# One transfer for the output projection's rows, a filler matmul, shared constants, and an uneven split of the result's columns in a gated decode step

## Chip, cores and metric

The kernel runs on one core of one Trainium2 chip. The metric is the device time of one execution in microseconds (us), as the median of several. A profiled execution gives the trace; its span, from the first to the last instruction, is about 1.5 us shorter than the device time. Every execution also has its span (to 0.1 us) recorded.

Engines: PE = TensorE matmul, PEld = its weight loads, DVE = VectorE, ACT = ScalarE, POOL = GpSimd, SPq = the queue of SyncE, which issues the transfers.

## The reference

```python
x = A_x                                              # (1, 1, 576), bf16
g = sigmoid((x * gate_w).sum(-1, keepdims=True))
# A: 32 query heads, 16 key/value heads, the last 4096 of 32768 positions
q = (x @ wq).reshape(1, 1, 32, 128).transpose(0, 2, 1, 3)
p = softmax(einsum("bhqd,bhkd->bhqk", q, k) * 128 ** -0.5)
a = einsum("bhqk,bhkd->bhqd", p, v) ... @ wo         # wo: (4096, 576)
# B: gelu MLP, hidden size 4608
b = gelu(x @ w1 + b1) @ w2 + b2                      # w2: (4608, 576)
return g * a + (1 - g) * b                           # (1, 1, 576), bf16
```

One token, so every weight and every cached key and value is read once and used once: 53.6 MB in, 1152 bytes out.

## The kernel before

Only what the change and the argument touch; `...` marks cuts. The result row of 576 columns accumulates in PSUM as two halves: `y_ps[0:1, ...]` and `y_ps[32:33, ...]`. `y_add` multiplies one vector by one row of `wo` or `w2` and issues a *pair* of matmuls, one for each half. There are 18 + 4 + 31 + 18 such rows: the first half of w2, a "tail" of four output rows, 31 main output rows, the second half of w2.

```python
DH = D // 2                                   # 288
one_b = const.tile([1, 2], BF16)              # a one, memset on POOL
...
xs_ps[:, i, :] <- lhsT=xdup[...], rhs=one_b[0:1, 0:1]     # nine matmuls, spread x over partitions
...
y_out = (y_ps[0:1, 0:DH], y_ps[32:33, 512 : 512 + DH])

def y_add(vec, row, start=False, stop=False):
    for s in range(2):
        last = nc.tensor.matmul(y_out[s], lhsT=vec, rhs=row[:, s * DH : (s + 1) * DH], ...)
    return last
...
for r0, r1 in ((0, 16), (16, RO)):            # RO = 31 rows for each of 128 partitions
    nc.sync.dma_start(out=wo_t[:, r0:r1, :]..., in_=wo_src[...][:, :, r0 * D : r1 * D])
for j0, j1 in ((0, 10), (10, 16), (16, 18)):
    nc.sync.dma_start(out=w2_t[:, NJ + j0 : NJ + j1, :], in_=w2_src[:, 1, j0:j1, :])
...
late = [(gt, f, w2_t[:, f, :]) for f in range(6, NJ)]
late += [(ov_tail, j, wo_tail[:, j, :]) for j in range(4)]
late += wo_at[0:8] + wo_at[16:RO] + wo_at[8:13] + w2_at[0:10] + wo_at[13:16] + w2_at[10:]
# every y_add is ordered behind the one before it
...
nc.scalar.copy(out=out_row[:, DH:D], in_=y_out[1])
nc.vector.tensor_copy(out=out_row[:, 0:DH], in_=y_out[0])
nc.sync.dma_start(out=out..., in_=out_row[:])
```

## Time and profile before

| | before |
|---|---|
| device time, first 3 runs | 131.78 us (131.72 to 132.05) |
| span of the profiled run | 130.1 us |
| busy: PE, DVE, ACT, POOL | 79.7, 52.3, 8.3, 9.2 us |
| bytes read, packets of the loads | 53.6 MB, 2490 |
| last packet of the loads ends | 127.50 us |
| PE ends, store issued | 128.4, 128.96 us |

To read it: add up no busy times. The loads fill their 16 engines for 96.5% of the span, so the table's last two rows are what counts: when the last bytes come, and what has to follow. The lines that show this stand in the prediction.

### The profile page before, as it was taken

Reading aid. Unit: us, or ns where it says so; the run is one execution under the profiler, and the core shown is the slowest. Engines: PE = TensorE matmul, PEld = TensorE weight load, DVE = VectorE, ACT = ScalarE, POOL = GpSimd, SP = SyncE. Lnnn points to the kernel's source line nnn. Section 1 sums busy time; section 2 is a strip of 40 time slices with the busy share of each in tenths; the row PEclk is TensorE's granted clock in tenths of the full one; section 3 lists DMA queues with packets and bytes.
Section 4 is the critical chain, followed back from the end, with each engine's and each line's share of the span. In section 5 each row is a group of like instructions: output and inputs, shape, how many; then the busy total and the mean of one; then the engine's idle time right before and its main releaser. Section 6 shows DMA issues by size and latency. Waiting matters only on the chain.

```text
span 130.1 us, 2403 instructions
## 1 busy us (share of the span) xinstructions
PE 79.7 (61%) x1148; PEld 45.6 (35%) x1077; DVE 52.3 (40%) x48; ACT 8.3 (6%) x18; POOL 9.2 (7%) x26
## 2 busy tenths in 40 slices
PE   0037999476003998939918994995300830899573
PEld 0037679375000121201211120595300830855441
DVE  0153000400079959999999995614000020010001
ACT  2000000003000000030003003011000000000001
POOL 7039700000000000000000000000000000000000
PEclk9999999999999999999997799985555555559999
DMA  6999999799899999999899899899899899999980
GB/s 232 427 431 432 476 424 476 344 484 448 373 458 453 403 433 463 393 433 484 373 433 484 383 423 484 357 432 505 368 433 489 363 438 415 442 401 427 413 363 33
DMA packets 2508, 53.75 MB, mean 413 GB/s; under 512 B 286, under 2 KB 290, under 8 KB 580
## 3 DMA queue, kind: packets, MB, share of 16 engines
q1 hardware_dynamic: 2490, 53.61, 96.5%
q8 instruction: 8, 0.13, 0.4%
q10 hardware_dynamic: 10, 0.01, 0.0%
HBM read 53.62 MB, written 0.00 MB: 412 GB/s over the span
## 4 chain that ended last, share of the span: by engine, by line
DMA 52%; DVE 24%; PE 14%; issue 6%; SPq 2%
DMA k_t<-in_A_k_cache_dram 27%; DMA w_t<-in_B_w_dram 25%; DVE kt L531 19%; PE s_ps L553 7%; PE o_ps L640 5%; DVE m L569 3%; DVE pt L602 2%; PE y_ps L396 1%; SPq L684 1%; DVE mr L572 1%; SPq L691 0%; DVE out_row L736 0%; SPq L234 0%; SPq L230 0%; PE mt_ps L578 0%
## 5 line engine op out<-in xcount | busy, mean ns | idle before, releaser
L553 PE MATMUL s_ps<-kt,qz_flat 128*128 128x512 bf16 x128 | 32.9, 414 | 17.2 <-DVE kt L531 10.4
L531 DVE STREAM_TRANSPOSE kt<-k_t 128x4096 f32<-128x4096 f32 x8 | 35.3, 4433 | 12.2 <-DMA k_t<-in_A_k_cache_dram 10.5
L640 PE MATMUL o_ps<-pt,v_t 128*128 128x8 bf16 x512 | 14.2, 168 | 16.6 <-DMA v_t<-in_A_v_cache_dram 14.7
L553 PEld LDWEIGHTS <-qz_flat 128*128 128x128 bf16 x64 | 6.9, 107 | 40.6 <-issue 40.4
L640 PEld LDWEIGHTS <-v_t 128*128 128x128 bf16 x512 | 14.0, 102 | 17.3 <-DMA v_t<-in_A_v_cache_dram 14.9
L424 PEld LDWEIGHTS <-w_t 128*128 128x128 bf16 x162 | 10.3, 167 | 1.8 <-issue 1.8
L424 PE MATMUL h_ps<-x,w_t 128*128 128x2 bf16 x162 | 10.5, 202 | 0.0
L590 ACT ACTIVATE p_t<-s_ps,negm 128x1024 bf16<-128x1024 f32 x4 | 4.5, 1114 | 50.9 <-DVE negm L586 50.9
L396 PE MATMUL y_ps<-w_t,gt 128*1 128x288 bf16 x72 | 6.3, 329 | 1.2 <-DMA w_t<-in_B_w_dram 1.2
L670 DVE RECIPROCAL rg<-mt_ps 128x32 f32<-128x32 f32 x1 | 0.4, 358 | 15.6 <-PE mt_ps L665 15.6
L602 DVE STREAM_TRANSPOSE pt<-p_t 128x1024 bf16<-128x1024 bf16 x4 | 4.9, 1225 | 2.7 <-ACT p_t L590 2.7
L462 PE MATMUL q_ps<-x,wq_t 128*128 128x2 bf16 x144 | 4.0, 166 | 2.9 <-DMA wq_t<-in_A_wq_dram 2.9
L569 DVE TENSOR_REDUCE m<-s_ps 128x1 f32<-128x1024 f32 x4 | 4.8, 1196 | 1.1 <-PE s_ps L553 1.1
L396 PE MATMUL y_ps<-wo_t,ov 128*1 128x288 bf16 x62 | 4.3, 285 | 1.4 <-DMA wo_t<-in_A_wo_dram 1.4
L736 DVE CAST out_row<-y_ps 1x288 bf16<-1x288 f32 x1 | 0.4, 445 | 11.6 <-PE y_ps L396 11.6
L433 DVE COPY hacc<-h_ps 128x36 f32<-128x36 f32 x1 | 0.2, 196 | 11.9 <-PE h_ps L424 11.9
L462 PEld LDWEIGHTS <-wq_t 128*128 128x128 bf16 x144 | 3.9, 104 | 3.0 <-DMA wq_t<-in_A_wq_dram 3.0
L345 PE MATMUL xs_ps<-one_b,rows 1*128 1x1 bf16 x9 | 0.7, 196 | 6.9 <-DVE rows L339 6.9
L396 PEld LDWEIGHTS <-gt 128*1 128x1 bf16 x72 | 3.3, 92 | 3.4 <-issue 1.6
L694 DVE TENSOR_TENSOR om<-o_ps,rgh 128x128 bf16<-128x128 f32 x1 | 0.3, 291 | 8.6 <-PE o_ps L640 8.6
L396 PEld LDWEIGHTS <-ov 128*1 128x1 bf16 x62 | 2.6, 83 | 2.8 <-issue 1.9
L339 DVE COPY rows<-rows 1x1152 bf16<-1x1152 bf16 x1 | 0.7, 748 | 6.1 <-DMA rows<-in_A_x_dram 6.1
(72 smaller groups left out, 35.5 us busy)
## 6 DMA issues: line engine op xcount, KB each, us to landing
k_t<-in_A_k_cache_dram SPq DMA_DIRECT2D x4, 4096.0 KB, 32.1
v_t<-in_A_v_cache_dram SPq DMA_DIRECT2D x4, 4096.0 KB, 22.8
wq_t<-in_A_wq_dram SPq DMA_DIRECT2D x1, 4608.0 KB, 25.8
w_t<-in_B_w_dram SPq DMA_DIRECT2D x1, 2880.0 KB, 14.1
w_t<-in_B_w_dram SPq DMA_DIRECT2D x1, 2592.0 KB, 22.9
w_t<-in_B_w_dram SPq DMA_DIRECT2D x1, 2304.0 KB, 8.1
wo_t<-in_A_wo_dram SPq DMA_DIRECT2D x1, 2304.0 KB
wo_t<-in_A_wo_dram SPq DMA_DIRECT2D x1, 2160.0 KB
```

Source lines behind the costliest of these rows:

```text
L339: nc.vector.tensor_copy(out=xdup.rearrange("p (d t) -> p d t", t=2), in_=x_row.rearrange("p (d o) -> p d o", o=1).to_broadcast([1, D, 2]),)
L396: last = nc.tensor.matmul(y_out[s], lhsT=vec, rhs=row[:, s * DH : (s + 1) * DH], start=start, stop=stop, skip_group_check=True,)
L424: nc.tensor.matmul(h_ps[:, j:NF:NJ], lhsT=w1_t[:, i, j:FH:NJ], rhs=x2[:, i, :], start=False, stop=(i == NI - 1 and j == NJ - 1), skip_grou ...
L462: nc.tensor.matmul(q_ps[:, j : Hq : Hq // 2], lhsT=wq_t[:, i, j * Dh : (j + 1) * Dh], rhs=x2[:, i, :], start=(i == 0 and j == 0), stop=(i ...
L531: lambda: nc.vector.transpose(out=kt[g, f][:].bitcast(FP32), in_=keys.rearrange("p c d -> p (c d)").bitcast(FP32),),
L553: last = nc.tensor.matmul(s_ps[g][:, u * 512 : (u + 1) * 512].rearrange("p (c k) -> p c k", k=32), lhsT=qz(g, j, 2 * f + half), rhs=kv[:, ...
L569: queue("dve", lambda: nc.vector.reduce_max(out=m1[:], in_=s_ps[g][:], axis=AX.X))
L572: lambda: nc.vector.tensor_scalar(out=mr[:], in0=hi16[:], scalar1=m1[:, 0:1], scalar2=None, op0=ALU.mult),
L590: nc.scalar.activation(out=p_t[:].rearrange("p c k -> p (c k)"), in_=s_ps[g][:], func=ACT.Exp, bias=negm[:, 0:1], scale=SCALE, accum_out=s ...
L602: lambda: nc.vector.transpose(out=pt[:, g, :, :].rearrange("p c q -> p (c q)"), in_=p_t[:].rearrange("p c k -> p (c k)"),),
L640: last = nc.tensor.matmul(o_ps[:, 8 * g : 8 * g + 8, 0], lhsT=v_t[g][:, c, :], rhs=pt[:, g, c % 32, 8 * (c // 32) : 8 * (c // 32) + 8], st ...
L684: nc.sync.dma_start(out=wo_t[:, r0:r1, :].rearrange("p r n -> p (r n)"), in_=wo_src[:, 0 : 4 * RW, :].rearrange("h (a r) n -> h a (r n)", ...
```

## The change

Its intent, as far as the code tells it: fewer and larger transfers, fewer small constants, and a smaller share for the VectorE, whose copy of 288 columns took 445 ns against the ScalarE's 390. The output rows come in one transfer, so they run as one block after it, and a dummy fp32 matmul (the filler) fills the place of the eight rows that used to run ahead.

```diff
-    DH = D // 2
+    DH = 272
...
-    one_b = const.tile([1, 2], BF16, name="one_b")
-    nc.gpsimd.memset(one_b[:], 1.0)
...
-    row_of = const.tile([HB, 16, HB, 2], BF16, name="row_of")
-    nc.gpsimd.memset(row_of[:], 0.0)
+    row_of = zeros[0:HB, ROWS : ROWS + 32 * HB].rearrange(...)     # part of the zeros tile
...
-            rhs=one_b[0:1, 0:1],
+            rhs=ident[0:1, 0:1],
...
-                rhs=row[:, s * DH : (s + 1) * DH],
+                rhs=row[:, DH:D] if s else row[:, 0:DH],
...
-    for r0, r1 in ((0, 16), (16, RO)):
-        nc.sync.dma_start(... r0 * D : r1 * D ...)
+    nc.sync.dma_start(out=wo_t..., in_=wo_src[:, 0 : 4 * RW, :]...)
...
-    late += wo_at[0:8] + wo_at[16:RO] + wo_at[8:13] + w2_at[0:10] + wo_at[13:16] + w2_at[10:]
+    spare_ps = ps_s.tile([P, 1024], FP32, name="spare_ps", tag="s")
+    late.append(None)                     # becomes one 128x512 fp32 matmul into spare_ps
+    late += wo_at + w2_at
```

More of the change, by code (lines that the diff above doesn't have):

```diff
@@ L265 @@
     NZ = 512 + 5 * RW + 1 + 64
-    zeros = const.tile([P, NZ + 4 * D], BF16, name="zeros")
+    ROWS = NZ + 4 * D
+    zeros = const.tile([P, ROWS + 32 * HB], BF16, name="zeros")
     nc.gpsimd.memset(zeros[:].bitcast(FP32), 0.0)
@@ L314 @@
     same8 = is0[:, c0 + 16 : NCC]
-    row_of = const.tile([HB, 16, HB, 2], BF16, name="row_of")
-    nc.gpsimd.memset(row_of[:], 0.0)
+    row_of = zeros[0:HB, ROWS : ROWS + 32 * HB].rearrange("p (r b m) -> p r b m", r=16, b=HB)
     nc.gpsimd.affine_select(
-        out=row_of[:],
-        in_=row_of[:],
+        out=row_of,
+        in_=row_of,
         pattern=[[0, 16], [-1, HB], [0, 2]],
@@ L391 @@
     y_ps = ps_y.tile([64, 1024], FP32, name="y_ps")
-    y_out = (y_ps[0:1, 0:DH], y_ps[32:33, 512 : 512 + DH])
+    y_out = (y_ps[0:1, 0:DH], y_ps[32:33, 512 : 512 + D - DH])
     def y_add(vec, row, start=False, stop=False):
@@ L541, in score_products @@
                     s_ps[g][:, u * 512 : (u + 1) * 512],
-                    lhsT=row_of[:].rearrange("p r b m -> p (r b m)"),
+                    lhsT=row_of.rearrange("p r b m -> p (r b m)"),
                     rhs=foreign[:].rearrange("p n b -> p (n b)"),
@@ L682 @@
     wo_t = big.tile([P, RO, D], BF16, name="wo_t", tag="D")
-    for r0, r1 in ((0, 16), (16, RO)):
-        nc.sync.dma_start(
-            out=wo_t[:, r0:r1, :].rearrange("p r n -> p (r n)"),
-            in_=wo_src[:, 0 : 4 * RW, :].rearrange("h (a r) n -> h a (r n)", a=4)[
-                :, :, r0 * D : r1 * D
-            ],
-        )
+    nc.sync.dma_start(
+        out=wo_t[:].rearrange("p r n -> p (r n)"),
+        in_=wo_src[:, 0 : 4 * RW, :].rearrange("h (a r) n -> h a (r n)", a=4),
+    )
     for j0, j1 in ((0, 10), (10, 16), (16, 18)):
@@ L727 @@
     late += [(ov_tail, j, wo_tail[:, j, :]) for j in range(4)]
-    late += wo_at[0:8] + wo_at[16:RO] + wo_at[8:13] + w2_at[0:10] + wo_at[13:16] + w2_at[10:]
+    spare_ps = ps_s.tile([P, 1024], FP32, name="spare_ps", tag="s")
+    late.append(None)
+    late += wo_at + w2_at
     before = ov_mm
-    for n, (vec, at, row) in enumerate(late):
+    for n, item in enumerate(late):
         with tc.issue_after(before.ins):
+            if item is None:
+                before = nc.tensor.matmul(
+                    spare_ps[:, 0:512],
+                    lhsT=ones[:],
+                    rhs=p_t[:].rearrange("p c k -> p (c k)").bitcast(FP32),
+                    start=True,
+                    stop=True,
+                )
+                continue
+            vec, at, row = item
             before = y_add(vec[:, at : at + 1], row, stop=(n == len(late) - 1))
```

## The prediction

> **What bounds the kernel now.** I read the page first, and on it the row of DMA shares. From the second slice to the last but one the 16 DMA engines are full, and one queue carries nearly everything:
>
> ```profile
> DMA  6999999799899999999899899899899899999980
> PEclk9999999999999999999997799985555555559999
> q1 hardware_dynamic: 2490, 53.61, 96.5%
> ```
>
> 53.61 MB on 16 engines that are 96.5% busy over a span of 130.1 us: whatever the compute engines do, the span cannot get much shorter than the bytes. So the kernel is bound by its transfers, and a change is worth what it does to the transfers, plus what it does behind the last one. The second row matters later: the granted matmul clock is half from about 88 to 117 us and full in the last four slices.
>
> Next the chain that ended last, in order of time, at its end. It says the same: a weight piece that had been waiting in the queue for 33 us, then sixteen matmuls and the copy of the result.
>
> ```profile
> 94.29 32.93 DMA w_t<-in_B_w_dram
> 127.22 0.04 issue
> 127.27 1.19 PE y_ps L396 x16
> 128.45 0.43 DVE out_row L736
> ```
>
> Third the timeline of the last 12 us, because the change reorders exactly these instructions:
>
> ```profile
> 118.58 0.65 PE L396 MATMUL y_ps<-zeros,ov_tail 48*1 48x288 bf16 x8
> 119.16 1.14 PE L396 MATMUL y_ps<-wo_t,ov 128*1 128x288 bf16 x16
> ...
> 121.72 2.61 PE L396 MATMUL y_ps<-wo_t,ov 128*1 128x288 bf16 x40 [1.42 <-DMA wo_t<-in_A_wo_dram]
> ...
> 125.18 1.39 PE L396 MATMUL y_ps<-w_t,gt 128*1 128x288 bf16 x20 [0.84 <-DMA w_t<-in_B_w_dram]
> ...
> 126.40 0.54 PE L396 MATMUL y_ps<-wo_t,ov 128*1 128x288 bf16 x6
> ...
> 127.27 1.15 PE L396 MATMUL y_ps<-w_t,gt 128*1 128x288 bf16 x16 [0.33 <-DMA w_t<-in_B_w_dram]
> ...
> 128.44 0.45 DVE L736 CAST out_row<-y_ps 1x288 bf16<-1x288 f32 x1 [11.62 <-PE y_ps L396]
> 128.48 0.39 ACT L735 CAST out_row<-y_ps 1x288 bf16<-1x288 f32 x1 [11.47 <-PE y_ps L396]
> 128.96 0.28 SPq L737 DMA_DIRECT2D out_dram<-out_row  x1
> ```
>
> Four idle gaps follow landings: the second half of the output projection at 121.72, the first w2 piece (ten rows) at 125.18, the second (six rows) at 127.27. The PE is not the bound here: it idles 1.42 + 0.84 + 0.33 = 2.59 us in the last 10.
>
> The trace also lists every packet. The last 2304-byte packet (third w2 piece, two rows) ends at 127.50 us. Packets of the three pieces before it end 0.48 to 0.50 us before the PE is let go (121.23 against 121.72, 124.68 against 125.18, 126.78 against 127.27), so the third piece is usable at about 127.99. The PE, starting six rows at 127.27, gets to its rows at 127.27 + 6 x 0.1225 = 128.00. Both are equally late: second and third piece bind together, within 0.01 us.
>
> **What the Trainium skill says.** "TensorE: Matmul & The Clock Gate", section "Back-to-back issue gap", gives N / 2.4 + 2.5 ns for one matmul at full clock, so 122.5 ns for 288 columns. The trace agrees for a *pair*: 20 pairs in 2.61 us is 20 x 122.5 ns plus 0.16 for the last to drain, 10 pairs in 1.39 and 8 in 1.15 fit with the same 0.16. The two matmuls of a pair therefore run at once; section "Part 3: Packing small matmuls — row/col tiling" of that page says outputs at partitions 0 and 32 fall in separate column groups, and that is how y_ps is laid out. Part 1 of the page says that the clock halves after an idle window of about 3.4 us; in this trace the step up comes at 117.6 us, 3 us into the burst that starts at 114.62. "DMA: Bandwidth & Descriptors", section "Rules for kernel authors", advises to coalesce small transfers, and says that below 64 KB one mostly pays overhead. The two halves merged here are 2304 and 2160 KB, so the advice gives almost nothing: 2304-byte packets take 94 ns and 32768-byte packets 1218 ns on average, which is 0.0369 ns per byte and about 9 ns fixed per packet.
>
> **The change part by part.** *One transfer for 31 rows.* Before: 128 packets of 18432 B and 128 of 17280 B; after: 128 of 35712 B, the same bytes. On each of 16 engines that is 8 packets fewer and one 4-byte semaphore packet fewer (those take 9 ns): 9 x 9 = 0.08 us off everything that lands behind. Issues are also fewer (0.58 us each), but the queue is 30 us ahead of the data, so that is hidden. I take 0.08 us off each landing: rows at 121.64, w2 pieces at 125.10, 127.19 and 127.91.
>
> *The order of the tail.* The eight output rows (16 matmuls) that ran at 119.16 now wait for the whole transfer, and a filler of 128x512 fp32 takes their place. After the landing the PE has 31 + 10 + 8 = 49 pairs.
>
> *The split 272 to 304.* A pair now lasts as long as its longer half: 304 / 2.4 + 2.5 = 129.2 ns (an estimate with the skill's formula that fitted above), 6.7 ns more. Walk: 121.64 + 31 x 0.1292 = 125.65 (first w2 piece long there); + 10 x 0.1292 = 126.94; wait for 127.19; + 6 x 0.1292 = 127.97 (third piece there at 127.91); + 2 x 0.1292 + 0.16 = 128.39. Before it was 128.42. So of the 49 x 6.7 = 0.33 us that the split costs, the eight last pairs' 0.05 lie on the path; the rest, and the eight rows moved back (8 x 0.129 = 1.03 us), eat the idle time of 0.84 + 0.33. What is left is 0.25 us.
>
> *The result's copies.* Slopes from this trace: DVE casts from PSUM take 190 ns for 31 columns and 445 for 288, so 1.0 ns a column; ACT 180 ns for 32 and 390 for 288, so 0.8. DVE gets 445 - 16 = 429, ACT 390 + 13 = 403. The ACT starts 0.04 later. Ends before: 128.89 and 128.87; after, relative to the same PE end: 128.87 and 128.88. Gain 0.01 us.
>
> *The constants.* The one-element operand of the first nine matmuls becomes the identity's corner. That is a new wait:
>
> ```profile
> 6.90 0.69 PE L345 MATMUL xs_ps<-one_b,rows 1*128 1x1 bf16 x9 [6.90 <-DVE rows L339]
> ...
> 9.34 0.29 POOL masks.py:199 TENSOR_SCALAR_AFFINE_SELECT ident<-ident 128x128 bf16<-128x128 bf16 x1
> ...
> 27.00 4.00 PE L462 MATMUL q_ps<-x,wq_t 128*128 128x2 bf16 x144 [2.87 <-DMA wq_t<-in_A_wq_dram]
> ```
>
> They now start at about 9.65 instead of 6.90. The bias matmuls that follow were at 10.49 and the w1 products at 11.70; nine matmuls (0.69) and the gate's (0.55) from 9.65 give 10.9 for the first and 12.2 for the second, some 0.5 us later. The PE then waits 2.87 us for wq at 24.13 to 27.00, which swallows it. The GpSimd saves two memsets (0.09 and 0.19 us) and spends about 0.06 on a wider one; nothing waits for them at the end.
>
> Sum: -0.03 at the PE end (0.08 off the landings, 0.05 back for wider pairs), -0.01 at the copies: 0.04 us. From 131.78 that is 131.74; as the best guess I take 131.70, since removing a boundary between transfers may also trim the spread between engines (the third w2 piece ends at 127.24 on the earliest of its sixteen last packets and 127.50 on the latest), which the packet sum does not count.
>
> **The rivals.** *The PE becomes the bound.* If the whole projection lands 0.25 us later relative to the w2 pieces, or a pair costs 135 instead of 129 ns, the slack of 0.25 us after 41 pairs is gone and each further 0.1 us shows in full. For it: 49 pairs now follow one landing. Against: the landing was measured for the last half, and the end of one transfer in ring order is the end of the same bytes. Time: 131.9 to 132.1.
>
> *The clock falls.* Without the filler the PE would idle from 119.2 to 121.6. If it went to half, pairs would take 304 / 1.2 = 253 ns for up to 3.4 us: 13 pairs' worth, about 1.7 us, less 0.25 slack: 133.2. Against: the filler. The fp32 bias pair of 576 columns took 1.12 us at 15.2 us, from which I estimate 1.0 to 1.9 us for the filler, so the idle is at most 1.5 us, as before (1.42), and the PE is busy for most of the time around it. Should the filler last 1.9 us from 119.4, it still ends at 121.3, ahead of the rows.
>
> *The transfer gain is real and larger*, for instance because the queue switches slowly between transfers. For it: nothing in the packet list; packets follow each other closely. It would make 131.3.
>
> **Range and chances.** The three runs before spread by 0.33 us, more than the effect. The mechanisms known add up to under 0.1 us, the two plausible surprises are +0.2 and -0.3. I give 131.70 with 131.35 to 132.00. A move by 2% is 2.6 us: only a fallen clock comes half that far. Faster 0.01, same 0.98, slower 0.01.
>
> **What would show it.** Right: in the new timeline the output rows run as one block of 62 matmuls at about 121.6 lasting 4.1 us, no idle before the first w2 piece's rows, a short wait (0.2 to 0.3) before the last sixteen, these lasting about 1.2 us; the last 2304-byte packets end under 0.1 us earlier; the clock stays full from 117.6 to the end; the q_ps block still starts at 27.0. Wrong: a wait of zero there and a later end (PE-bound), a half clock after 120 us, or landings that move by over 0.2 us.

## The result

| | before | changed | ratio of the fast runs |
|---|---|---|---|
| first series, 6 runs each | 131.80 us (131.64 to 132.05) | 131.68 us (131.52 to 131.88) | 0.9991, 95% interval 0.9978 to 1.0004 |

"Same", and inside the range of 131.35 to 132.00; the point was 131.70. A ratio is the mean time of one kernel's fast runs over that of the other's of the same rounds, so not quite the ratio of the medians beside it.

The page of the changed kernel, its clock row and its main queue. There are 144 packets fewer (2346 for 2490) and the same bytes:

```profile
PEclk9999999999999999999995899975555555555999
q1 hardware_dynamic: 2346, 53.61, 96.4%
```

The chain that ended last (start, duration, what), at its end. It has the shape of the one before: a w2 piece, sixteen matmuls, a copy. But the last copy is now the ScalarE's:

```profile
94.69 32.72 DMA w_t<-in_B_w_dram
127.41 0.04 issue
127.45 1.21 PE y_ps L394 x16
...
128.69 0.40 ACT out_row L742
```

The timeline of the last 13 us (start, duration, engine, line, what):

```profile
116.85 3.20 PE L394 MATMUL y_ps<-w_t,gt 128*1 128x272 bf16 x24
...
119.98 0.75 PE L394 MATMUL y_ps<-zeros,ov_tail 48*1 48x272 bf16 x8
...
120.66 1.13 PE L730 MATMUL spare_ps<-p_t,ones 128*128 128x512 f32 x2
...
121.90 3.78 PE L394 MATMUL y_ps<-wo_t,ov 128*1 128x272 bf16 x59
...
125.49 0.28 PE L394 MATMUL y_ps<-w_t,gt 128*1 128x272 bf16 x1
125.52 0.29 PE L394 MATMUL y_ps<-wo_t,ov 128*1 128x304 bf16 x1
...
128.57 0.43 DVE L743 CAST out_row<-y_ps 1x272 bf16<-1x272 f32 x1 [11.43 <-PE y_ps L394]
128.69 0.40 ACT L742 CAST out_row<-y_ps 1x304 bf16<-1x304 f32 x1 [11.35 <-PE y_ps L394]
129.12 0.28 SPq L744 DMA_DIRECT2D out_dram<-out_row  x1
```

And the groups of that stretch with shapes kept apart (count, then busy us and mean ns of one):

```profile
L394 PE MATMUL y_ps<-wo_t,ov 128*1 128x304 bf16 x31 | 4.2, 292 | 0.0
L394 PE MATMUL y_ps<-wo_t,ov 128*1 128x272 bf16 x31 | 3.8, 279 | 0.1
```

Four things to see. First, the long idle gaps before the output rows and before the first w2 piece are gone; the wait that is left is the one at 127.45. Second, the two halves of the row run at their own pace: 31 matmuls of 272 columns are busy for 3.8 us, 31 of 304 for 4.2, and a w2 matmul of the narrow half starts at 125.49, ahead of output-row matmuls of the wide half (125.52) that come before it in program order. The lead has a limit: the narrow half never starts more than four rows ahead, and its last two rows before the wait go at the wide half's 0.129 us instead of 0.116. Third, the copies therefore start 0.12 us apart and the ScalarE's ends last: 128.57 + 0.43 = 129.00 against 128.69 + 0.40 = 129.09. Fourth, the clock stepped up at 120.17 us, not at 117.57 as in the trace before, so the filler ran at 120.66 to 121.79, right up to the rows.

The span of this profile is 0.2 us longer than that of before, while its time in the series is 0.1 us shorter. The last packet of the loads ends at 127.62 against 127.50. Over nine profiles of kernels with the one transfer (the changed kernel three times, and six profiles of variants below that leave the loads alone) this end lies between 127.47 and 127.69. That is the trace's own spread, over twice the effect in question; so single profiles tell mechanisms here, not 0.1 us.

### The profile page after: what moved, and what is told of

Its sections match the earlier page's. It is cut to its first block, busy times and chain, and to the rows that moved or that the text cites. A ratio compares the mean times of both kernels' runs of the same rounds, so it can differ in the third digit from the quotient of the medians.

```text
span 130.3 us, 2402 instructions
## 1 busy us (share of the span) xinstructions
PE 81.5 (63%) x1150; PEld 47.8 (37%) x1080; DVE 52.0 (40%) x48; ACT 8.3 (6%) x18; POOL 9.1 (7%) x24
## 2 busy tenths in 40 slices
DMA packets 2364, 53.75 MB, mean 413 GB/s; under 512 B 270, under 2 KB 274, under 8 KB 564
## 3 DMA queue, kind: packets, MB, share of 16 engines
q1 hardware_dynamic: 2346, 53.61, 96.4%
## 4 chain that ended last, share of the span: by engine, by line
DMA 52%; DVE 24%; PE 13%; issue 6%; SPq 2%; ACT 0%
DMA k_t<-in_A_k_cache_dram 27%; DMA w_t<-in_B_w_dram 25%; DVE kt L529 19%; PE s_ps L551 7%; PE o_ps L638 5%; DVE m L567 3%; DVE pt L600 2%; SPq L686 1%; PE y_ps L394 1%; DVE mr L570 1%; SPq L681 0%; PE mt_ps L576 0%; SPq L234 0%; ACT out_row L742 0%; SPq L230 0%
## 5 line engine op out<-in xcount | busy, mean ns | idle before, releaser
L551 PE MATMUL s_ps<-kt,qz_flat 128*128 128x512 bf16 x128 | 32.4, 410 | 17.4 <-DVE kt L529 10.6
L394 PE MATMUL y_ps<-w_t,gt 128*1 128x272 bf16 (+1 forms) x72 | 8.0, 363 | 0.1
L343 PE MATMUL xs_ps<-ident,rows 1*128 1x1 bf16 x9 | 0.6, 189 | 9.4 <-POOL ident masks.py:199 9.4
L394 PEld LDWEIGHTS <-gt 128*1 128x1 bf16 x72 | 4.5, 97 | 2.2 <-issue 0.7
L394 PE MATMUL y_ps<-wo_t,ov 128*1 128x272 bf16 (+1 forms) x62 | 4.2, 286 | 0.1
L343 PEld LDWEIGHTS <-rows 1*128 1x128 bf16 x9 | 0.7, 150 | 9.3 <-DVE rows L337 6.6
L394 PEld LDWEIGHTS <-ov 128*1 128x1 bf16 x62 | 3.4, 84 | 1.3 <-issue 0.8
```

The source lines that it names most:

```text
L343: nc.tensor.matmul(xs_ps[:, i, :], lhsT=xdup[:, i : 2 * D : NI], rhs=ident[0:1, 0:1], start=(i == 0), stop=(i == NI - 1), skip_group_check ...
L394: last = nc.tensor.matmul(y_out[s], lhsT=vec, rhs=row[:, DH:D] if s else row[:, 0:DH], start=start, stop=stop, skip_group_check=True,)
L551: last = nc.tensor.matmul(s_ps[g][:, u * 512 : (u + 1) * 512].rearrange("p (c k) -> p c k", k=32), lhsT=qz(g, j, 2 * f + half), rhs=kv[:, ...
```

## The experiments

Twelve experiments with nine different kernels, in three jobs on three chips, five rounds each, all correct. "Before" and the ratios below are of the kernel before in the same job. The three series of the changed kernel against the kernel before:

| series | changed, median | before, median | ratio, 95% interval |
|---|---|---|---|
| first | 131.68 us | 131.80 us | 0.9991 (0.9978 to 1.0004) |
| control | 131.73 us | 131.78 us | 0.9992 (0.9974 to 1.0009) |
| control_2 | 131.69 us | 131.72 us | 0.9990 (0.9976 to 1.0005) |

**control** and **control_2**: no edit.

> The changed kernel once more, for a second profile and a tighter interval. Theory (the transfers bind the end, one boundary less is worth 0.08 us, the wider pairs cost back 0.05): ratio to the kernel before 0.9995 to 1.000. Rival (the boundary between two transfers is worth more than its packets): 0.997 or less. The landing of the last w2 piece varies by 0.1 us from profile to profile, and the clock step up falls where its 3.4 us grid lies.

> The changed kernel once more, beside the next three on one chip. Spans of 130.1 to 130.4 us in all six runs; with the filler no run shows a span over 131.

Three series agree on 0.1% less by their means, 0.12 us, and none excludes zero. By the medians it is 0.12, 0.05 and 0.03 us; the means of the kernel before hold a few long times (132.12 to 132.32) whose spans are ordinary (130.2 to 130.5). The spans of control_2 are 130.1 to 130.4, of control 130.2 to 130.3; none of the 17 runs is above 131. The small gain fits the packet count but is not shown by timing; the next two runs enlarge its cause instead.

### What a packet costs

**row_packets**: one transfer for the output rows as changed; the four w2 transfers are rewritten, as the program is finished, to one run per row.

```diff
 src, dst = i.ins[0], i.outs[0]          # of each w2 load: 128 partitions x (rows * 576)
+rows_ap = [[D, size // D], [1, D]]
+ins=[copy.replace(src, ap=[src.ap[0]] + rows_ap)], outs=[copy.replace(dst, ap=[dst.ap[0]] + rows_ap)]
```

> One transfer for the output rows as changed, but the four w2 transfers cut into packets of one row (1152 B): 288 packets on each engine in place of 32, no transfer more. Theory: 256 x 9 ns = 2.3 us over the changed kernel, all at the landing of the last piece. Rival (packets of over 512 B are free): nothing.

**eight_transfers** and **two_transfers**:

```diff
-    nc.sync.dma_start(out=wo_t..., in_=wo_src...)
+    for r0, r1 in ((0, 4), (4, 8), ..., (24, 28), (28, RO)):     # two_transfers: ((0, 16), (16, RO))
+        nc.sync.dma_start(out=wo_t[:, r0:r1, :]..., in_=...[:, :, r0 * D : r1 * D])
```

> The output rows in eight transfers (seven of 4 rows, one of 3): 56 data packets and 7 semaphore packets more on each engine than in one. Theory: 63 x 9 ns = 0.57 us over the changed kernel. Rival (cost sits in the boundary, say 0.2 us each): 1.4 us or more. Rival (hidden): nothing.

> The changed kernel with the output rows in two transfers again (16 and 15 rows), order, filler and split as changed. Theory (9 ns a packet, 9 packets more on each engine): 0.08 us over the changed kernel. Rival (a boundary costs more than its packets): 0.3 us or more.

| | median | before | ratio, 95% interval |
|---|---|---|---|
| two_transfers | 131.75 us | 131.70 us | 1.0002 (0.9990 to 1.0014) |
| eight_transfers | 132.22 us | 131.70 us | 1.0037 (1.0024 to 1.0050) |
| row_packets | 133.88 us | 131.70 us | 1.0174 (1.0159 to 1.0188) |

The page of row_packets shows that the edit did what it should: 4096 packets more than the 2364 of the changed kernel, the same bytes.

```profile
DMA packets 6460, 53.75 MB, mean 406 GB/s; under 512 B 270, under 2 KB 4882, under 8 KB 4916
```

From two transfers to eight there are 48 data and 6 semaphore packets more on each engine: 54 x 9 ns = 0.49 us; measured 132.22 - 131.75 = 0.47. From two_transfers to row_packets there are 256 - 9 = 247 more: 2.2 us; measured 2.13. So the boundaries between transfers show no price beyond their packets (to about 0.2 us for six of them, which is what the intervals resolve), packets of over 1 KB are not free, and what the loads lose the time loses in full. So the one transfer should be worth 9 x 9 = 0.08 us. Against two_transfers the changed kernel's ratio in its first series, another job, is 0.0011 lower (0.14 us), with intervals that overlap: compatible, not resolved.

**one_w1**: the same gain sought at the other end of the queue, as a version that might beat both kernels.

```diff
-    for i0, i1 in ((0, 4), (4, NI)):
+    for i0, i1 in ((0, NI),):
         nc.sync.dma_start(out=w1_t[:, i0:i1, :], in_=w1_src[:, i0:i1, :])
```

> The changed kernel with the w1 rows in one transfer instead of two (128 packets of 41472 B in place of 128 of 18432 and 128 of 23040). Theory (9 packets less on each engine, 9 ns each, at the start of a queue that never runs dry): 0.08 us less than the changed kernel, and the w1 products start at about 15 instead of 11.5 and end at about 25.3, still ahead of wq at 27.0. Rival (the late start of the products reaches the end): 0.3 us or more over it.

131.72 us, ratio 0.9995 (0.9982 to 1.0008), spans 130.2 to 130.4: as the changed kernel. My expectation of the products was wrong, for they started at 20.21 us and ended at 30.4, not at 25.3, and ran past the landing of wq. Yet nothing reached the end: the copies of the queries (qz_flat) ended at 35.96 us and the score products that need them started at 41.35, so even then the early chain had over 5 us of room. A gain of 0.08 us isn't visible, nor excluded.

### The shared constant

**own_one**:

```diff
+    one_b = const.tile([1, 2], BF16, name="one_b")
+    nc.gpsimd.memset(one_b[:], 1.0)
-            rhs=ident[0:1, 0:1],
+            rhs=one_b[0:1, 0:1],
```

> The changed kernel with the one-element constant given back to the first nine matmuls. Theory: they start at 6.6 us instead of 9.4, the q_ps block still starts at 27.0, and the time is that of the changed kernel within 0.05 us. Rival (the early chain reaches the end): 0.3 us or more less.

131.69 us, the changed kernel's median within 0.05 us as expected; ratio 1.0009 (0.9992 to 1.0026), with one run of 132.39 whose span is ordinary (130.4). Timeline lines, first of the changed kernel, then of own_one:

```profile
9.40 0.64 PE L343 MATMUL xs_ps<-ident,rows 1*128 1x1 bf16 x9 [9.40 <-POOL ident masks.py:199]
26.97 4.00 PE L460 MATMUL q_ps<-x,wq_t 128*128 128x2 bf16 x144 [2.95 <-DMA wq_t<-in_A_wq_dram]
```

```profile
7.30 0.69 PE L345 MATMUL xs_ps<-one_b,rows 1*128 1x1 bf16 x9 [7.30 <-DVE rows L339]
26.89 4.00 PE L462 MATMUL q_ps<-x,wq_t 128*128 128x2 bf16 x144 [2.45 <-DMA wq_t<-in_A_wq_dram]
```

The shared constant costs 2.1 us of waiting at the start, and the wait for wq swallows all of it. The move of `row_of` into the zeros tile was not tested by itself; it changes GpSimd work before 15.2 us, in front of the same wait.

### The split

**wide_split**:

```diff
-    DH = 272
+    DH = 224
```

> The changed kernel with columns 224 to 352. Theory (a pair lasts as long as its longer half, 352 / 2.4 + 2.5 = 149 ns): 49 pairs from 121.85 us end at 129.3 instead of 128.65, with 0.04 us more for the copy: 0.6 to 0.7 us over the control, and the wait before the last sixteen matmuls is gone in the ScalarE's half. Rival (a pair lasts as the mean of its halves): no change.

132.68 us (132.36 to 133.51), ratio 1.0071 (1.0044 to 1.0098). Three of six runs lie at 132.36 to 132.52, 0.6 to 0.8 over the control's 131.73; three at 132.85 to 133.51. The profile is of the second sort (132.98):

```profile
121.35 1.12 PE L730 MATMUL spare_ps<-p_t,ones 128*128 128x512 f32 x2
...
129.77 0.38 DVE L743 CAST out_row<-y_ps 1x224 bf16<-1x224 f32 x1 [12.43 <-PE y_ps L394]
129.91 0.44 ACT L742 CAST out_row<-y_ps 1x352 bf16<-1x352 f32 x1 [12.38 <-PE y_ps L394]
```

Its clock stepped up only at 120.61 us, the longer pairs had made the work before late, and the filler held the PE until 122.40, when the rows had long landed (last packet 121.33). From there 49 x 0.1492 + 0.16 us give 129.87 for the wide half, and its copy starts at 129.91. So the longer half sets the end, the mean does not, and with no slack left each delay shows in full. The narrow half went at 96 ns a row for twelve rows, until it was four rows ahead, and from there at the wide half's 149 ns.

**even_split**, run twice:

```diff
-    DH = 272
+    DH = D // 2
```

> The changed kernel with columns 288 to 288. Theory: the two column groups run at their own pace, the end waits for the slower; with 288 the ScalarE's half ends 8 x 6.7 = 0.05 us earlier behind the last wait, so 0.05 us less than the control (ratio to it 0.9996), and the two copies start within 0.05 us of each other instead of 0.12. Rival (the split serves its purpose): 0.05 us more than the control.

> 288 to 288 again, because the first time its four ordinary runs were 0.13 us over the control, which its trace does not explain: from the last wait of the PE to the end of the later copy both take 1.62 us (0.05 us less matmul, 0.05 us more for the VectorE's copy). Theory now: equal, medians within 0.06 us of control_2. Rival (the split gains 0.1 us): again 0.1 or more over it.

First series 131.89 us, ratio 1.0025 (0.9991 to 1.0059); second 131.86 (131.82 by its fast runs), ratio 1.0015 (0.9985 to 1.0046). The first expectation, 0.05 us *less* than the control, fell: the median is 0.16 us over it. The second, within 0.06 us of control_2, missed too: 0.13 us over it by the fast runs, as the rival said. The first trace gives no reason for such a difference:

```profile
127.50 1.15 PE L394 MATMUL y_ps<-w_t,gt 128*1 128x288 bf16 x16 [0.37 <-DMA w_t<-in_B_w_dram]
...
128.68 0.45 DVE L743 CAST out_row<-y_ps 1x288 bf16<-1x288 f32 x1 [11.59 <-PE y_ps L394]
128.72 0.39 ACT L742 CAST out_row<-y_ps 1x288 bf16<-1x288 f32 x1 [11.43 <-PE y_ps L394]
```

From the wait's end to the end of the later copy it is 129.13 - 127.50 = 1.63 us here, 129.09 - 127.45 = 1.64 with 272 to 304, and 128.89 - 127.27 = 1.62 in the kernel before. What the narrow half gains for the VectorE, the wide half's matmuls take. So the trace argues for no effect, and the timing neither shows nor excludes that the uneven split gains 0.1 us: the ordinary runs of the second series (131.58 to 131.89) lie as control_2's (131.56 to 131.82), those of the first (131.80 to 131.89) above the control's (131.67 to 131.77), and the intervals overlap.

The second series' profiled run is slow (134.22) and is no measure of the split. But its trace shows where this one run lost its time, and it was not in the loads, whose last packet ended at 127.49:

```profile
121.22 2.07 PE L730 MATMUL spare_ps<-p_t,ones 128*128 128x512 f32 x2
...
123.22 5.16 PE L394 MATMUL y_ps<-wo_t,ov 128*1 128x288 bf16 x62
```

Its clock stood at half until 125.71 us. At half clock the filler took 2.07 us instead of 1.13 and held the output rows until 123.22, while their last packet had come at 121.21.

Two other runs of the twelve were long: 133.31 and 132.95, with spans of 131.9 and 131.5 us. They pull the ratios up. They were not profiled, so whether the clock did it there too is not known. The changed kernel has no such run in 17; whether 288 columns make them likelier stays open with three cases.

### The filler

**no_filler**, run twice:

```diff
-    spare_ps = ps_s.tile([P, 1024], FP32, name="spare_ps", tag="s")
-    late.append(None)
```

> The changed kernel without the 128x512 fp32 filler. Theory: the idle before the output rows is 1 to 2.5 us, under one 3.4 us window, the clock stays full or has just risen, and the end is set by the transfers: within 0.1 us of the control. Rival (the filler is needed): the clock is half after 121.8 us, 62 matmuls take 6 to 8 us instead of 4.1, and the time is 1 to 1.7 us longer.

> Without the filler again, for the share of runs in which the clock falls. The first time 2 of 6 runs had a span of 131.5 and more, and the one that was profiled shows the clock at half from 122.24 to 125.66. Theory now (the idle of 1.6 us is shorter than a 3.4 us grid cell, so a fall depends on where the grid lies): again some of the six runs at 131.4 to 131.7, the rest at 130.1 to 130.4. Rival (chance of that job): all six under 130.6.

First series 131.77 us (131.62 to 133.06), second 132.33 us (131.49 to 133.44); ratios 1.0022 (0.9984 to 1.0061) and 1.0046 (1.0002 to 1.0091). My first expectation was right for seven of the twelve runs (spans 130.1 to 130.4) and wrong for five (131.5, 131.5, 131.6, 131.6, 132.0). The profile of the first series caught one of the five. Its timeline, and its stretches of 1 us (busy PE, PEld, DVE, ACT, POOL, then granted clock, DMA share, GB/s):

```profile
119.55 0.68 PE L394 MATMUL y_ps<-zeros,ov_tail 48*1 48x272 bf16 x8
...
121.82 5.45 PE L394 MATMUL y_ps<-wo_t,ov 128*1 128x272 bf16 x59 [1.59 <-DMA wo_t<-in_A_wo_dram]
```

```profile
121.00:122.00 1.00, 0.18 (x4) 0.15 (x5) 0.00 (x0) 0.00 (x0) 0.00 (x0) 1.00 1.10 454
122.00:123.00 1.00, 1.00 (x15) 0.92 (x13) 0.00 (x0) 0.00 (x0) 0.00 (x0) 0.62 0.91 371
123.00:124.00 1.00, 1.00 (x12) 0.67 (x10) 0.00 (x0) 0.00 (x0) 0.00 (x0) 0.50 0.99 417
124.00:125.00 1.00, 1.00 (x12) 0.90 (x10) 0.00 (x0) 0.00 (x0) 0.00 (x0) 0.50 0.92 383
125.00:126.00 1.00, 1.00 (x15) 0.74 (x12) 0.00 (x0) 0.00 (x0) 0.00 (x0) 0.67 0.97 396
```

The clock records give the steps: up at 118.83 us, down at 122.24, up at 125.66, at distances of 3.41 us. In the first of these cells the PE had been busy for about 1.8 us and idle for 1.59; right after the rows had landed the clock halved for one whole cell, and the rows took 5.45 us instead of 3.78. That is beyond the slack, and the time rises by 1.3 us. The second series' profile shows the same, with the fall at 122.12. With the filler, in the first trace of even_split, a cell that lies alike (118.44 to 121.85) had about 2.4 us busy and about 1.0 idle, and the clock held. Five of 12 against none of 17 is no chance result in my judgement, and both traces without the filler show the fall itself. The kernel before, with the old order and no filler, has no span over 130.6 in the 33 runs of these three jobs.

Two limits. The filler is no full guard: the 288-column kernel has it too, and its slow trace above stayed at half clock until 125.71 us all the same. And busy time alone does not decide a fall: in the changed kernel's own trace the cell from 126.99 to 130.41 us held only about 1.6 us of matmuls, and the clock records show no fall up to their end at 132.0. What in a cell decides stays open.

## Why the prediction was right

It was right in the time, the range and the main mechanism; some steps were not. That its point lies 0.02 us from the median is luck: the six runs spread by 0.36 us, and the last 0.04 us of the point (a smaller spread between engines) had no working; in the trace after, the sixteen last packets end over 0.41 us, not less than the 0.27 before.

- *The transfers bind, and 9 ns a packet is the currency.* Shown by the two dose runs: 0.47 us for an estimated 0.49, and 2.13 for 2.2. The term of 0.08 us itself is too small to be seen alone, and the sign that was named for it, last packets under 0.1 us earlier, did not come in the first trace (127.62 against 127.50).
- *The slack of the PE is 0.25 us.* In the trace after, the wide half gets through 41 rows at 121.90 + 41 x 0.1292 = 127.20 and goes on at 127.45: again 0.25 (0.16 and 0.27 in the two controls). wide_split shows the end of that slack.
- *The moment of the rows was off.* They were put at 121.64; in the trace after they began at 121.90, in the two controls at 122.01 and 121.99. The last packet ends at 121.34 to 121.41 in these three against 121.23 before; over the nine profiles it lies between 121.19 and 121.41, so this is the spread of the loads, and in control the filler was still running then (120.95 to 122.07). The w2 pieces moved with the rows, so the slack survived.
- *"A pair lasts as long as its longer half"* holds for the wide half only. The narrow half runs ahead, up to four rows, at 272 / 2.4 + 2.5 = 115.8 ns a row: its first w2 matmul starts 3.59 us after the first of its 31 rows, which is 31 x 115.8. That broke the step on the copies: they were to end at 128.87 and 128.88, as if both started from one PE end; in fact they ended 0.09 us apart, at 129.00 and 129.09. The estimated gain of 0.01 us there wasn't seen (1.64 us against 1.62 from the last wait).
- *"The clock stays full from 117.6"* failed: the step came at 120.17. The prediction dated it to 3 us into a burst from 114.62, but in that trace the PE had been busy without a gap since 111.11, and in the one after since 111.36; that reading could not place the step. The 24 matmuls after 116.85 took 3.20 us in place of 2.13, and the wait for the rows absorbed it with 0.1 us to spare (the filler ended at 121.79, the rows began at 121.90).
- *The rival of the fallen clock* was taken as improbable because of the filler, and put at 133.2 us. Without the filler it did come, in five of twelve runs, at 132.90 to 133.44. So the order that the change needs cost 1.3 us in some runs without the filler. With it the changed kernel had no such run in 17, but three runs of twelve with 288 columns were long in spite of it: the rival was less remote than it was taken to be.
- *The constants* did as predicted at the first matmuls and at the wait: 9.40 for an estimated 9.65, q_ps at 26.97 for 27.00. Between them the delay of 0.5 us did not come: the bias matmuls started at 10.38 and the w1 products at 11.53, for an estimated 10.9 and 12.2 (10.49 and 11.70 before).
- *A slip:* the prediction counts four idle gaps after landings; its lines show the three that it names.

Where the gain that the change aimed at went: the merged transfer is worth its packets and no more, the split, by its trace, gives to one copy what it takes in the other half's matmuls, and the constants lie in front of a wait for data. No version clearly better than the changed kernel was found.

## What to carry to other kernels

In a kernel bound by its loads, count packets per engine before merging transfers: at the 9 ns each seen here, nine fewer on each engine are worth less than the noise, while four loads cut into runs of 1152 B cost 1.7%. Before an output is split unevenly between two engines, follow each part from the last wait through its own matmuls to the end of its own copy; the balance lies where those sums meet, not where the copies do. And when work is moved behind a late load, look at what the clock sees in the gap left behind, over many runs, since the median of the first six runs hid a loss that two of them had.

## What the Trainium skill lacked or had wrong

- "DMA: Bandwidth & Descriptors", "Rules for kernel authors" and "Why small descriptors are slow (HBM only)": no time per packet is given for loads issued by SyncE (the second section counts about three cycles of an internal bus for each, and the page has a time only for loads issued by GpSimd), and coalescing is advised for transfers under 64 KB. Here each packet costs about 9 ns beside 0.037 ns a byte, at 17 KB still about 11 (648.7 ns for 17280 B), and 247 packets more per engine cost 2.13 us.
- "TensorE: Matmul & The Clock Gate", "Part 3": it says that matmuls keep program order in start and end. In the changed kernel's trace two column groups drift apart, by up to four rows: a 272-column matmul starts at 125.49 us, 304-column ones that precede it in the program at 125.52 and later (starts as recorded; ends in this profile are modelled and prove nothing).
- The same page, "Why this matters for your kernels" and Part 1: gaps of over about 3 us are named as the danger. Here the clock fell after one gap of 1.59 us, when a 3.41 us cell held about 1.8 us of PE work. With about 2.4 us it held, but with about 1.6 us in another trace (after, 126.99 to 130.41) it held as well, so no rule comes out of these runs.
- No page says that a filler can delay the work that it was to speed up. In the slow run of even_split_2, at half clock, it took 2.07 us and held the rows until 123.22, with their last packet in at 121.21; in wide_split the half clock until 120.61 made it late, and it held the rows until 122.40, last packet at 121.33. In the traces in which the PE waits for the rows it starts 0.5 to 0.6 us after that packet.
